# Soft-capped attention before two MLPs on one core: scores made with the keys on the partitions by two row tiles, exp with no row maximum, key sums by matmuls

## The chip, the cores and the metric

The kernel runs on 1 core of one Trainium2 chip. The metric is the device time of one execution in microseconds (us), the median over runs. The engines are TensorE (PE in the profile; PEld is its weight load), VectorE (DVE), ScalarE (ACT), GpSimd (POOL) and SyncE (SP, which issues most of the DMAs).

## The reference

Attention over 4 batches, 12 heads, 448 tokens and a head size of 64, in float32; then one MLP with relu squared and one with x·sigmoid(1.702x), both 768 → 2048 → 768, on the 1792 tokens. `cap` is 30; the weights are float64.

```python
scores = scale * np.matmul(q, k.transpose(0, 1, 3, 2))
scores = cap * np.tanh(scores / cap)
scores = scores - np.max(scores, axis=-1, keepdims=True)
attn = np.exp(scores)
attn = attn / (np.sum(attn, axis=-1, keepdims=True) + 1e-09)
x = np.matmul(attn, v)                      # heads side by side: [1792, 768]
h = np.maximum(x @ w_in, 0.0);  x = h * h @ w_out
h = x @ w_in2;  out = (h * (1.0 / (1.0 + np.exp(-1.702 * h)))) @ w_out2
```

## The kernel before, in words

A float32 operand is split as hi + lo in the type float32r, and a product of two such operands is three float32r matmuls (hi·hi, hi·lo, lo·hi), or two where one side's halves lie side by side.

**Attention** goes by pairs of heads (24 pairs, 6 for each batch). q and k of a pair are transposed to [64 x 2 heads, tokens], by TensorE for batches 0 and 1 and by VectorE's 32x32 transposes for batches 2 and 3 (`DVE_QK`). k's halves are written once for each head and copied to the other 64 partitions by a DMA on GpSimd's queue (`prep_k`, step 3), so that a score matmul contracts over 128 rows: q's hi and lo of one head against k's hi, and again against k's lo. `scores` puts the queries on the partitions (112 at a time). ScalarE takes tanh out of PSUM (`tanhs`), VectorE takes each row's maximum (`row_max`), ScalarE takes exp of 448 elements at a time with the maximum as bias and the row sum as accumulated output (`exps`), VectorE divides by the sum (`norm`). TensorE then transposes the probabilities (`trans`, 16 transposes for a head, four of them with 64 output partitions), ScalarE and VectorE take them from PSUM and split them (`take`), and `pv` multiplies with v. For batch 0 (`PLAIN_PV`) that product is left in float32.

**The MLPs** go by units of work n: 68 units for a batch, each one product of 15 or 18 matmuls of 448 columns (`product`), in all 1152 matmuls for a batch. The weights come as float64 halves in batch 0, are brought to float32 by ScalarE (`rebias`) and VectorE (`join`), written back to DRAM by SP (`keep`), and split by both (`split_w`). Later batches read `keep`.

**The order.** `HEAD_PLAN` and `PAIR_PLAN` say in which quarter slot of a head a step is issued; `attn_sub(t)` issues one quarter slot. The attention of batch 0 stands alone, ahead of the first product; that of batch s + 1 is issued between the units of batch s. Each engine then works its instructions off in order. SP's queue takes the loads of q, k, v, the weights and the `keep` writes in the order of issue.

Of the kernel before, what the change touches and what calls it, by code (L numbers as in the profile page):

```python
# [8 lines left out]
F32 = mybir.dt.float32  # L9
F32R = mybir.dt.float32r  # L10
I32 = mybir.dt.int32
U8 = mybir.dt.uint8
# [9 lines left out]
def softcap_attention_mlp_mlp(ctx, tc, q, k, v, cap, w1, w2, w3, w4, out):  # L22
    """Soft-capped attention, then a relu^2 MLP, then a x*sigmoid(1.702x) MLP.

    The weights are float64 and come as the int32 halves of their words. They are brought to
    float32 on chip once and kept in DRAM for the later batches.

    A float32 operand x is split exactly into x = hi + lo with hi = float32r(x), and a product is
    the sum of the float32r products hi*hi + hi*lo + lo*hi.

    """
# [14 lines left out]
    # batches whose product with v is left in float32  # L46
# [6 lines left out]
    # batches whose q and k are transposed on the vector engine  # L53
    DVE_QK = (2, 3)
    # pairs whose scores are left in float32
# [54 lines left out]
    def emit_const():  # L110
        nc.sync.dma_start(out=capt, in_=cap.rearrange("(o n) -> o n", o=1).to_broadcast([P, 1]))
        make_identity(nc, ident)
        for t in sx:
            nc.gpsimd.memset(t, 0)
        # tanh is odd: cap and -cap give the same scores
        nc.vector.tensor_scalar(ncap, capt, -1.0, None, ALU.mult)
        nc.vector.tensor_tensor(acap, capt, ncap, ALU.max)
        nc.vector.tensor_scalar(ncap, acap, -1.0, None, ALU.mult)
        nc.vector.reciprocal(qs, acap)
        nc.vector.tensor_scalar(qs, qs, float(D) ** -0.5, None, ALU.mult)  # L120

# [5 lines left out]
    def load_pair(b, p):  # L127
        if b in DVE_QK:
            # blocks of 32 x 32, which the vector engine transposes in place
            qt = ld.tile([P, S // 32, 32], F32, tag="q", name="qt")  # L130
            kt = ld.tile([P, S // 32, 32], F32, tag="k", name="kt")
            for t, src in ((kt, k), (qt, q)):
                for j in range(4):
                    Q_LOAD.dma_start(
                        out=t[32 * j : 32 * j + 32],
                        in_=src[b, 2 * p + j // 2, :, 32 * (j % 2) : 32 * (j % 2) + 32].rearrange(
                            "(c p) d -> p c d", p=32
                        ),
                    )
        else:  # L140
            qt = ld.tile([CP, NCH, 2, D], F32, tag="q", name="qt")
            kt = ld.tile([CP, NCH, 2, D], F32, tag="k", name="kt")
            for t, src in ((kt, k), (qt, q)):
                for j in range(2):
                    Q_LOAD.dma_start(
                        out=t[:, :, j, :], in_=src[b, 2 * p + j].rearrange("(p c) d -> p c d", c=NCH)
                    )
        raw[b, p] = (qt, kt)

    def transposed(b, t, name):  # L150
        """[64 x 2 heads, tokens] of a pair's q or k."""
# [11 lines left out]
    def load_v(b, p):  # L163
        plain = b in PLAIN_PV
        if plain:
            # [v_even | 0 | v_odd], so that both heads of a pair add into one bank
# [16 lines left out]
    def split_v(b, p, half):  # L183
        if b in PLAIN_PV:
            return
        if half == 0:
            # [hi_even | lo_even | lo_odd | hi_odd]
# [123 lines left out]
    def take(b, h, half):  # L311
        """The transposed probabilities from PSUM."""
# [86 lines left out]
    # a quarter slot's work: what feeds an operation was made a quarter slot or more before  # L399
# [46 lines left out]
    def ready(b):  # L446
        """The quarter slot that ends the attention of batch b, and leaves ps_x free."""
        return 4 * (H * (b + 1) - 1) + LAST_HEAD + 1

# [1 line left out]
    layer = []  # L451
    for l, (wa, wb) in enumerate(((w1, w2), (w3, w4))):
# [11 lines left out]
        # the next group's first product stands ahead of a group's second ones  # L464
# [31 lines left out]
    def words(n, t):  # L496
        """A unit's raw words without their two lowest bytes, in elements of type t."""
        return wraw[n][:, : units[n][5], :].bitcast(t).rearrange("p k (f e) -> p k f e", f=P)

    def rebias(n):  # L500
        """float64 to float32, first part: the upper 13 bits.

        The upper 16 bits of a float64 are taken as a bfloat16 and cast to float16, which loses the
        three upper bits of the exponent: what is left are the upper 16 bits of the float32, the last
        three of them zero.
        """
# [5 lines left out]
    def join(n):  # L512
        """float64 to float32, second part: the lower 19 bits of the fraction."""
# [43 lines left out]
    def finish(n, part):  # L557
        """What follows a product, in two parts."""
# [3 lines left out]
        if kind == "a":  # L562
            if part == 0:
# [8 lines left out]
                else:  # L572
                    # h * sigmoid(1.702 h) = 0.5 h (1 + tanh(0.851 h)); the 0.5 comes at the end
# [9 lines left out]
        if part == 0:  # L583
# [4 lines left out]
            # the 0.5 of the second MLP's activation  # L588
# [28 lines left out]
    def ahead(n):  # L617
        """The weights' way ahead of unit n."""
# [5 lines left out]
    def urgent(n):  # L624
        """Whether the unit after n takes what n gives."""
# [50 lines left out]

# [28 lines left out]
```

## Time and profile before

| | us |
|---|---|
| median of 3 runs (1248.27 to 1251.95) | 1249.37 |
| the profiled execution, first to last instruction (its span) | 1247.7 |
| PE busy / DVE busy / ACT busy in the span | 1211.9 / 929.9 / 834.8 |

Only the span of the profiled execution is known; the median is 1.7 us longer than it. I cut the span where a batch's products begin and end:

| stage | from to (us) | what runs |
|---|---|---|
| A | 0 to 128.4 | attention of batch 0, and the first pairs of batch 1 |
| B | 128.4 to 430.1 | MLPs of batch 0, attention of batch 1, weights from float64 |
| C | 430.1 to 722.5 | MLPs of batch 1, attention of batch 2 |
| D | 722.5 to 1007.1 | MLPs of batch 2, attention of batch 3 |
| E | 1007.1 to 1247.7 | MLPs of batch 3, alone |

A matmul's duration in the profile (about 0.37 us) is longer than the distance from one to the next (about 0.205 us), because matmuls follow each other through the array. So PE's busy time says little of how much work it has; the distances between starts do.

### The profile page before, as it was taken

To read this page: it belongs to the slowest core of one execution; us is meant where nothing else is said; L and a number is where in the kernel's file an instruction comes from. 1 tells how busy PE (TensorE), PEld (TensorE's weight loads), DVE (VectorE), ACT (ScalarE), POOL (GpSimd) and SP (SyncE) were. 2 spreads that over 40 slices of the span, in tenths; PEclk is the share of its full clock that TensorE was granted. 3 is DMA by queue.
4 is the path that set the end of the run, shared out by engine and by line. 5 is a ranking of instruction groups with operands and counts; after the bars stand their busy time and mean duration, and the time that the engine had idled before them with its cause. 6 is when DMAs were issued, how large, how long until landed. Compare 5 with 4: busy or idle time off the path is not lost.

```text
span 1247.7 us, 17463 instructions
## 1 busy us (share of the span) xinstructions
PE 1211.9 (97%) x6192; PEld 1096.6 (88%) x6192; DVE 929.9 (75%) x1497; ACT 834.8 (67%) x1459; POOL 74.7 (6%) x140
## 2 busy tenths in 40 slices
PE   4998999989999999999999999999999999999997
PEld 3676898879999999999999999999999999999997
DVE  5999987979989986789768876778745663565354
ACT  6999988888987776677766847667654443344332
POOL 2000000000000310000000130000000130000000
PEclk9999999989999999999999999999999999999999
DMA  6734898879888864334334353232222243233232
GB/s 149 196 68 128 268 285 235 273 210 296 243 280 246 264 166 120 110 100 138 116 88 127 94 163 109 71 100 102 77 93 93 99 151 109 98 114 120 97 108 50
DMA packets 188039, 185.67 MB, mean 149 GB/s; under 512 B 109744, under 2 KB 158896, under 8 KB 187952
## 3 DMA queue, kind: packets, MB, share of 16 engines
q1 hardware_dynamic: 177776, 168.72, 44.4%
q0 software_dynamic: 4608, 15.15, 4.8%
q10 hardware_dynamic: 5568, 0.69, 0.3%
q8 instruction: 49, 0.80, 0.3%
q14 instruction: 38, 0.31, 0.1%
HBM read 142.84 MB, written 30.67 MB: 139 GB/s over the span
## 4 chain that ended last, share of the span: by engine, by line
PE 81%; DVE 7%; ACT 6%; DMA 3%; issue 1%; SPq 0%; DVEq 0%; ACTq 0%
PE mps L552 68%; PE tps L305 5%; PE sps L257 4%; PE vps L370 3%; DMA wraw<-in_moe_w_out_dram 2%; ACT e L284 2%; DVE st L278 1%; DVE e L295 1%; ACT sx L510 1%; PE vps L365 1%; DVE y L517 1%; ACT wh L534 1%; DVE qq L240 1%; DVE wl L536 1%; DMA wraw<-in_moe_w_in_dram 1%
## 5 line engine op out<-in xcount | busy, mean ns | idle before, releaser
L552 PE MATMUL mps<-g,wh 128*128 128x448 f32 x1536 | 443.6, 370 | 6.0 <-ACT g L579 4.0
L552 PE MATMUL mps<-xt,wh 128*128 128x448 f32 x1536 | 440.7, 368 | 2.5 <-ACT wh L534 2.5
L534 ACT ACTIVATE wh<-wraw 128x768 fp32r<-128x768 f32 (+1 forms) x204 | 164.6, 807 | 263.1 <-PE mps L552 237.1
L552 PEld LDWEIGHTS mps<-g,wh 128*128 128x128 f32 x1536 | 287.5, 189 | 32.4 <-ACT g L579 4.7
L552 PEld LDWEIGHTS mps<-xt,wh 128*128 128x128 f32 x1536 | 286.5, 188 | 26.4 <-ACT wh L534 2.7
L536 DVE TENSOR_TENSOR wl<-wraw,wh 128x768 fp32r<-128x768 f32 (+1 forms) x204 | 185.0, 907 | 160.6 <-ACT wh L534 157.3
L552 PE MATMUL mps<-g,wl 128*128 128x448 f32 x768 | 282.0, 367 | 1.0 <-DVE wl L536 1.0
L552 PE MATMUL mps<-xt,wl 128*128 128x448 f32 x768 | 281.0, 366 | 0.0
L284 ACT ACTIVATE e<-e,st,acap 112x448 f32<-112x448 f32 x192 | 144.1, 752 | 20.2 <-DVE st L280 19.8
L552 PEld LDWEIGHTS mps<-g,wl 128*128 128x128 f32 x768 | 144.9, 189 | 13.5 <-DVE wl L536 1.4
L552 PEld LDWEIGHTS mps<-xt,wl 128*128 128x128 f32 x768 | 144.2, 188 | 12.1
L579 ACT ACTIVATE g<-r 128x448 fp32r<-128x448 f32 x128 | 73.6, 575 | 56.1 <-DVE r L575 29.5
L305 PEld LDWEIGHTS tps<-ident,e 112*128 112x128 f32 (+1 forms) x768 | 98.2, 183 | 12.5 <-ACT e L273 4.2
L278 DVE TENSOR_REDUCE st<-e 112x2 f32<-112x896 f32 x96 | 103.0, 1079 | 7.8 <-ACT e L273 7.5
L257 PE MATMUL sps<-kk,qq 128*112 128x448 f32 x384 | 101.5, 387 | 6.4 <-DVE qq L240 2.1
L305 PE MATMUL tps<-ident,e 112*128 112x112 f32 (+1 forms) x768 | 103.7, 276 | 1.5 <-ACT e L273 1.1
L581 DVE TENSOR_TENSOR g<-r,g 128x448 fp32r<-128x448 f32 x128 | 79.4, 620 | 32.2 <-ACT g L579 31.5
L593 DVE SCALAR_TENSOR_TENSOR y<-mps,y 128x448 f32<-128x448 f32 x96 | 59.5, 619 | 53.1 <-PE mps L552 52.4
L273 ACT ACTIVATE e<-sps 112x896 f32<-112x896 f32 x96 | 87.3, 912 | 9.2 <-PE sps L257 7.1
L257 PEld LDWEIGHTS sps<-kk,qq 128*112 128x112 f32 x384 | 67.0, 179 | 22.6 <-ACT e L273 4.1
L510 ACT ACTIVATE sx<-wraw 128x768 f16<-128x768 bf16 (+1 forms) x68 | 69.8, 1029 | 19.2 <-DMA wraw<-in_moe_w_out_dram 9.1
L295 DVE TENSOR_SCALAR e<-e,st 112x448 f32<-112x448 f32 x192 | 78.7, 450 | 1.7
(73 smaller groups left out, 1150.9 us busy)
## 6 DMA issues: line engine op xcount, KB each, us to landing
wraw<-keep SPq DMA_DIRECT2D x66, 768.0 KB, 4.3
wraw<-in_moe_w_in_dram SPq DMA_DIRECT2D x32, 766.5 KB, 5.7
wraw<-keep SPq DMA_DIRECT2D x36, 640.0 KB, 4.3
keep<-y SPq DMA_DIRECT2D x44, 384.0 KB, 3.4
wraw<-in_moe_w_out_dram SPq DMA_DIRECT2D x24, 638.8 KB, 5.5
kk<-kk POOLq DMA_DIRECT2D x48, 224.0 KB, 3.6
wraw<-in_moe_w_out_dram SPq DMA_DIRECT2D x12, 766.5 KB, 6.3
keep<-y SPq DMA_DIRECT2D x24, 320.0 KB, 3.1
```

Source lines behind the costliest of these rows:

```text
L257: nc.tensor.matmul(ps[:CP, u, :S], qq[:, j, c * CP : (c + 1) * CP], kk[:, j, i, :], start=(i == 0), stop=(i == 1),)
L273: nc.scalar.activation(e[:, 2 * half : 2 * half + 2, :], ps[:CP, :, :S], AF.Tanh)
L278: nc.vector.tensor_reduce(st[:, 0, cs], e[:, cs, :], axis=AX.X, op=ALU.max)
L284: nc.scalar.activation(e[:, c, :], e[:, c, :], AF.Exp, scale=acap[:CP], bias=st[:, 1, c : c + 1], accum_out=st[:, 2, c : c + 1],)
L295: nc.vector.tensor_scalar(e[:, c, :], e[:, c, :], st[:, 3, c : c + 1], None, ALU.mult)
L305: nc.tensor.transpose(ps[:n, u, c * CP : (c + 1) * CP], e[:, c, cols], ident[:CP, :CP])
L510: nc.scalar.activation(z, words(n, BF16)[:, :, :, 2], AF.Copy)
L534: nc.scalar.activation(hi[:, :kn], t[:, :kn], AF.Copy)
L536: eng.tensor_tensor(lo[:, :kn], t[:, :kn], f32(hi[:, :kn]), ALU.subtract)
L552: nc.tensor.matmul(ps[:, :S], a[:, kk, :], r, start=(kk == 0 and i == 0), stop=(kk == kn - 1 and i == 2),)
L579: nc.scalar.activation(g[:, 0, :], r, AF.Copy)
L581: eng.tensor_tensor(g[:, 1, :], r, f32(g[:, 0, :]), ALU.subtract)
```

## The change

The old kernel stays as a function `any_cap`, for caps over 40. A new function `bounded_cap` computes the same for caps up to 40, and a branch at the end runs `any_cap` as well if the cap is larger (here it is 30, so the branch is not taken). In `bounded_cap`:

- `scores` puts the keys on the partitions and the queries along the columns, for both heads of a pair. Each matmul contracts over the 64 rows of one head: the even head's lie in rows 0 to 63 of the array, the odd head's in rows 64 to 127, and they write to two PSUM banks. Three products (hi·hi, hi·lo, lo·hi) for each head and chunk of 112 keys make 6 matmuls for each `scores` call and 24 for a pair. The copy of k to the other partitions is gone.
- `exps` takes exp with no maximum, 896 elements at a time. `row_max`, `norm`, `trans` and `take` are gone: the probabilities already lie as `pv` wants them, and are split there (`split_hi`, `split_lo`).
- The sums over the keys are matmuls with a column of ones, for batch 0 from every chunk (`PE_SUMS`), for the others from the chunks added up on VectorE (`add_keys`). Their reciprocals are spread over the 64 rows of a head by another matmul and multiplied to the product with v (`recip`, `normalize`).
- q and k of batch 1 are transposed on VectorE too, and v is split in all batches.

```diff
+    DVE_QK = (1, 2, 3)
+    PE_SUMS = (0,)
+    NORM = {0: [(0, 3), (3, 5), (5, 6)]}
+    DVE_HI = {0: (0, 2)}
...
+    def scores(b, p, c):
+
+        qq, kk = prep[b, p]
+        ps = sc[b, p, c] = ps_s.tile([P, 2, 512], F32, tag="s", name="sps")
+        for i, (ik, iq) in enumerate(((0, 0), (0, 1), (1, 0))):
+            for j in range(2):
+                r = slice(64 * j, 64 * j + 64)
+                nc.tensor.matmul(
+                    ps[:CP, j, :S], kk[r, ik, c * CP : (c + 1) * CP], qq[r, iq, :],
+                    start=(i == 0), stop=(i == 2),
+                )
+
+    def tanhs(b, p, c):
+        e = et[b, p, c] = e_p.tile([CP, 2, S], F32, tag="e", name="e")
+        nc.scalar.activation(e, sc.pop((b, p, c))[:CP, :, :S], AF.Tanh)
+
+    def exps(b, p, c):
+        e = et[b, p, c]
+        nc.scalar.activation(e, e, AF.Exp, scale=ecap[:CP])
+
+    def split_hi(b, p, c):
...
+        if c in DVE_HI.get(b, ()):
+            nc.vector.tensor_copy(hi, e)
+        else:
+            nc.scalar.activation(hi, e, AF.Copy)
+
+    def split_lo(b, p, c):
+        hi, lo = hl[b, p, c]
+        nc.vector.tensor_tensor(lo, et[b, p, c], f32(hi), ALU.subtract)
+
+    def add_keys(b, p, c):
...
+        nc.vector.tensor_tensor(a, et[b, p, 0] if c == 1 else a, et[b, p, c], ALU.add)
+
+    def key_sum(b, p, c):
...
+        for j in range(2):
+            w = one[:CP, P - 1 - row - j : 2 * P - 1 - row - j]
+            for n, t in enumerate((hi, lo)):
+                nc.tensor.matmul(
+                    ps[:, :S], w, t[:, j, :],
+                    start=first and j == 0 and n == 0, stop=last and j == 1 and n == 1,
+                )
+
+    def pv(b, p, c):
...
+        for j in range(2):
+            a = vt[:, c, 2 * j : 2 * j + 2, :].rearrange("p a d -> p (a d)")
+            for n, t in enumerate((hi, lo)):
+                nc.tensor.matmul(
+                    pvp[b, p][j][:, :S], a, t[:, j, :],
+                    start=(c == 0 and n == 0), stop=(c == NCH - 1 and n == 1),
+                )
+        if b in PE_SUMS:
+            key_sum(b, p, c)
...
+    def recip(b, p, step):
...
+            nc.vector.reciprocal(sums[r], sums[r])
+        elif step == 1:
+            nc.scalar.activation(rcp[r, 0, :], sums[r], AF.Copy)
+        elif step == 2:
+            nc.vector.tensor_tensor(rcp[r, 1, :], sums[r], f32(rcp[r, 0, :]), ALU.subtract)
+
+    def normalize(b, p, k):
...
+            for m in range(2):
+                nc.tensor.matmul(
+                    ps[:, u, :S],
+                    spread[n - p0].rearrange("p j d -> p (j d)"),
+                    rcp[:, m, :],
...
+            x = x32[b, n]
+            nc.vector.tensor_tensor(x, x, ps[:, u, :S], ALU.mult)
+            if b == 0:
+                split_x(b, n)
...
+        11: [(sum_hi,)],
+        12: [(take_x, 0), (take_x, 1), (sum_lo,), (recip, 0)],
+        13: [(sum_keys,), (recip, 1)],
+        14: [(take_sums,), (recip, 2)],
+        15: [(recip, 3)],
+        16: [(recip, 4)],
+        17: [(normalize, 0)],
+        18: [(normalize, 2)],
+        19: [(normalize, 4)],
+    }
+    for c in range(NCH):
+        for i, f in enumerate((scores, tanhs, exps, split_hi, split_lo, pv)):
+            PLAN.setdefault(2 * c + i, []).append((f, c))
+        PLAN[2 * c + 4].append((add_keys, c))
...
+    nc.sync.dma_start(out=c[:, 0:1], in_=cap.rearrange("(o n) -> o n", o=1))
...
+    nc.vector.tensor_scalar(over, c[:, 0:1], CAP_MAX, None, ALU.is_gt)
+    bounded_cap(tc, q, k, v, cap, w1, w2, w3, w4, out)
+    flag = nc.values_load(over, min_val=0, max_val=1)
+    with tc.If(flag > 0):
+        any_cap(tc, q, k, v, cap, w1, w2, w3, w4, out)
```

The order of TensorE's matmuls in stage B, at a place where attention stands between the products (`mps`) of batch 0's MLPs; before, with `vps` the product with v, `tps` the transposed probabilities and `qps` q transposed:

```order
L552 MATMUL mps<-g,wl 128x448
L158 MATMUL qps<-ident,qt 128x112 x4
L370 MATMUL vps<-pb,vs 128x448 x2
L370 MATMUL vps<-pc,vs 128x448
L305 MATMUL tps<-ident,e 128x112 x4
L305 MATMUL tps<-ident,e 64x112 x4
L552 MATMUL mps<-g,wh 128x448 x2
```

And now, with `sps` the scores and `sums` the sums over the keys (the product is line 1185, the scores line 888):

```order
L1185 MATMUL mps<-g,wl 128x448
L888 MATMUL sps<-qq,kk 112x448 x6
L956 MATMUL vps<-phi,vs 128x448
L956 MATMUL vps<-plo,vs 128x448
L956 MATMUL vps<-phi,vs 128x448
L956 MATMUL vps<-plo,vs 128x448
L888 MATMUL sps<-qq,kk 112x448 x6
L942 MATMUL sums<-phi,one 128x448
L1185 MATMUL mps<-g,wh 128x448 x2
```

The transposes are gone from between the products; a run of 6 score matmuls, each on half of the array's rows, and matmuls on all 128 rows take turns.

The order of ScalarE's instructions late in stage A; before, with line 273 the tanh, line 284 the exp, 337 a copy of transposed probabilities, 396 the split of x, 215 and 191 the splits of k and v:

```order
L284 ACTIVATE e,st<-e,st,acap 112x448
L273 ACTIVATE e<-sps 112x896
L284 ACTIVATE e,st<-e,st,acap 112x448
L396 ACTIVATE xt<-x_1046 128x448
L337 ACTIVATE pb<-tps 128x448
L215 ACTIVATE kk<-kps 64x448 x2
L191 ACTIVATE vs<-vraw 128x4x2x64
L273 ACTIVATE e<-sps 112x896
L284 ACTIVATE e,st<-e,st,acap 112x448 x3
```

And now, with line 895 the tanh, 899 the exp, 909 the hi half of the probabilities, 974 the product with v taken from PSUM, 1014 the hi half of the reciprocals:

```order
L895 ACTIVATE e<-sps 112x896
L974 ACTIVATE ct<-vps 64x448 x2
L899 ACTIVATE e<-e,ecap 112x896
L895 ACTIVATE e<-sps 112x896
L909 ACTIVATE phi<-e 112x896
L899 ACTIVATE e<-e,ecap 112x896
L895 ACTIVATE e<-sps 112x896
L862 ACTIVATE kk<-kps 128x448
L899 ACTIVATE e<-e,ecap 112x896
L1014 ACTIVATE rcp<-sums 4x448
```

There is one exp for 896 elements where there were two of 448, and it waits for the tanh alone, where before it waited for VectorE's maximum; the copies of the transposed probabilities are gone, the hi halves and the copies `ct` are new.

## Rows read from the trace of the kernel before

**Rows 1.** The page: engines' busy time, and the chain that ended last.

```profile
PE 1211.9 (97%) x6192; PEld 1096.6 (88%) x6192; DVE 929.9 (75%) x1497; ACT 834.8 (67%) x1459; POOL 74.7 (6%) x140
PE 81%; DVE 7%; ACT 6%; DMA 3%; issue 1%; SPq 0%; DVEq 0%; ACTq 0%
```

**Rows 2.** Busy time by stretch: 40 us within stage A, then stages A to E.

```profile
core 0: us, PE busy (x) PEld busy (x) DVE busy (x) ACT busy (x) POOL busy (x), PEclk, DMA share, GB/s
40.00:80.00 40.00, 38.84 (x203) 27.75 (x202) 39.00 (x78) 39.70 (x80) 4.32 (x12) 1.00 0.48 115
0.00:128.40 128.40, 104.87 (x517) 76.92 (x517) 111.31 (x214) 114.44 (x221) 13.77 (x38) 0.96 0.54 136
128.40:430.10 301.70, 295.74 (x1529) 271.50 (x1529) 268.98 (x420) 257.82 (x437) 13.74 (x24) 0.99 0.85 262
430.10:722.50 292.40, 292.40 (x1526) 270.09 (x1525) 232.96 (x387) 201.46 (x364) 21.47 (x36) 1.00 0.43 121
722.50:1007.10 284.60, 284.60 (x1475) 262.29 (x1474) 196.29 (x309) 166.87 (x292) 18.19 (x30) 1.00 0.31 101
1007.10:1247.70 240.60, 234.31 (x1153) 215.81 (x1151) 120.36 (x170) 94.19 (x148) 7.51 (x12) 1.00 0.33 104
```

**Rows 3.** Products alone (line 552), in stages B to D together and in E.

```profile
128.40:1007.10 878.70, 736.58 (x3454) 645.92 (x3455) 1.00 0.54 163
1007.10:1247.70 240.60, 234.31 (x1153) 215.81 (x1151) 1.00 0.33 104
```

**Rows 4.** Stages B to D, line by line: scores (L257), transposed probabilities (L305), product with v (L370).

```profile
128.40:1007.10 878.70, 62.35 (x256) 44.46 (x256) 1.00 0.54 163
128.40:1007.10 878.70, 70.61 (x551) 69.35 (x550) 1.00 0.54 163
128.40:1007.10 878.70, 67.44 (x245) 45.79 (x245) 1.00 0.54 163
```

**Rows 5.** Timeline of PE in stages C and D: start, us, then the instructions.

```profile
692.53 1.07 PE L305 MATMUL tps<-ident,e 112*128 112x112 f32 x8
693.38 0.64 PE L552 MATMUL mps<-xt,wh 128*128 128x448 f32 x2
...
766.66 0.37 PE L552 MATMUL mps<-g,wl 128*128 128x448 f32 x1
766.86 0.98 PE L257 MATMUL sps<-kk,qq 128*112 128x448 f32 x4
767.68 0.57 PE L552 MATMUL mps<-g,wh 128*128 128x448 f32 x2
```

**Rows 6.** Timeline where transposes into 64 columns of the array end and products begin.

```profile
605.25 0.77 PE L305 MATMUL tps<-ident,e 112*128 112x112 f32 x6
605.37 0.42 PEld L305 LDWEIGHTS tps<-ident,e 112*64 112x64 f32 x4
...
605.80 0.65 PE L552 MATMUL mps<-xt,wh 128*128 128x448 f32 x2
```

**Rows 7.** Groups of ScalarE's and VectorE's instructions over the span, shapes apart.

```profile
L284 ACT ACTIVATE e<-e,st,acap 112x448 f32<-112x448 f32 x192 | 144.1, 752 | 20.2 <-DVE st L280 19.8
L278 DVE TENSOR_REDUCE st<-e 112x2 f32<-112x896 f32 x96 | 103.0, 1079 | 7.8 <-ACT e L273 7.5
L273 ACT ACTIVATE e<-sps 112x896 f32<-112x896 f32 x96 | 87.3, 912 | 9.2 <-PE sps L257 7.1
L284 ACT ACTIVATION_READ_ACCUMULATOR e<-e,st,acap 112x1 f32 x192 | 36.5, 190 | 0.0
L534 ACT ACTIVATE wh<-y 128x768 fp32r<-128x768 f32 x44 | 36.8, 836 | 3.4 <-PE mps L552 1.6 <-DVE y L517 0.9 <-ACT pc L342 0.8
L536 DVE TENSOR_TENSOR wl<-y,wh 128x768 fp32r<-128x768 f32 x44 | 41.9, 952 | 6.1 <-ACT wh L534 5.8
L579 ACT ACTIVATE g<-r 128x448 fp32r<-128x448 f32 x128 | 73.6, 575 | 56.1 <-DVE r L575 29.5 <-DVE r L571 25.8
L581 DVE TENSOR_TENSOR g<-r,g 128x448 fp32r<-128x448 f32 x128 | 79.4, 620 | 32.2 <-ACT g L579 31.5
```

More of the change, by code (lines that the diff above doesn't have):

```diff
@@ L21, in softcap_attention_mlp_mlp, with any_cap @@
 @with_exitstack
-def softcap_attention_mlp_mlp(ctx, tc, q, k, v, cap, w1, w2, w3, w4, out):
+def any_cap(ctx, tc, q, k, v, cap, w1, w2, w3, w4, out):
     nc = tc.nc
@@ new lines, with softcap_attention_mlp_mlp @@
+CAP_MAX = 40.0
+@with_exitstack
+def softcap_attention_mlp_mlp(ctx, tc, q, k, v, cap, w1, w2, w3, w4, out):
+    nc = tc.nc
+    pool = ctx.enter_context(tc.tile_pool(name="flag", bufs=1))
+    c = pool.tile([1, 2], F32, name="capsize")
+    over = pool.tile([1, 1], I32, name="over")
+    nc.sync.dma_start(out=c[:, 0:1], in_=cap.rearrange("(o n) -> o n", o=1))
+    nc.vector.tensor_scalar(c[:, 1:2], c[:, 0:1], -1.0, None, ALU.mult)
+    nc.vector.tensor_tensor(c[:, 0:1], c[:, 0:1], c[:, 1:2], ALU.max)
+    nc.vector.tensor_scalar(over, c[:, 0:1], CAP_MAX, None, ALU.is_gt)
[3 more added lines that the diff above has]
+        any_cap(tc, q, k, v, cap, w1, w2, w3, w4, out)
```

445 lines of the change are left out of this document (added).

## The prediction

> **What bounds the kernel now.** I read the page first: PE is busy 97% of the span, and 81% of the chain that ended last is PE [rows 1]. An average over stages with different limits says little, so next come the busy times by stretch [rows 2]. In stage A two other engines are full: in 40 us of it ACT is busy 39.7 and DVE 39.0. A lasts 128.4 us, of which ACT works 114.4 and waits 14.0, mostly while the first loads come. In C and D PE never idles, with DVE at 69 to 80% and ACT lower: there each PE instruction removed is time gained. B is PE's as well but for 6 us of idleness; its DMA share of 0.85 is the next limit. E is products alone.
>
> The price of a product comes from E: 234.3 us for 1153 matmuls, 0.2032 us each [rows 3]. In B to D the 3454 products cost 702 us of 878.7. The attention between them is 256 score matmuls, 551 transposes and 245 matmuls with v [rows 4]. From one start to the next, four scores take 0.82 us (0.205 each) and eight transposes 0.85 us (0.106 each) [rows 5]; with v at 0.205 that makes 52.5 + 58.4 + 50.2 = 161.1 us. The remaining 15 us are waits, q and k transposes, and stretches at the lower clock.
>
> **Stages B to D: PE.** The built program, in its order of issue, has 402 score matmuls behind the fifth product, and 392 full-height ones: 282 with v, 72 sums, 38 that spread reciprocals. The 392 have a known shape, 392 × 0.205 = 80.4 us. The transposes are gone. The 402 are of a kind that the trace doesn't show: 64 rows each, in pairs for the two halves of the array. Bounds: if the halves work at once, a pair can't be faster than one matmul's 0.205 us; if they take turns, a pair takes 0.41. For the issue of two weight loads and two matmuls the nearest row is the transposes, each a load and a matmul in 0.106 us, so 0.21 for two. I take 0.22 for a pair: 201 × 0.22 = 44.2 us.
>
> A rule on packing would put it higher. The Trainium skill (TensorE: Matmul & The Clock Gate, section Measured speedup vs the span model) gives 3.07 times for four row tiles; by the same share of the ideal two would take an estimated 0.27 us a pair, and the whole forecast would be 10 us longer. No row here shows it.
>
> The runs of scores and the full-height matmuls change the way the array is divided 141 times behind the fifth product. The nearest row is the change from transposes into 64 columns of the array back to products: the first product starts at 605.80, while the transposes before it end at 605.25 + 0.77 = 606.02 [rows 6]. So the array wasn't emptied first. I take 0.025 us for a change, 3.5 us; the upper bound is that the array empties each time, 0.37 − 0.205 = 0.165 us, by the length of a matmul less its distance [rows 5].
>
> B to D then hold 44.2 + 80.4 + 3.5 = 128.1 us of attention instead of 161.1: **−33 us**, between −40 and +2 by the bounds of the pair. The 15 us of waits I leave. In B the DMA engines bound this: 0.85 × 301.7 = 256 us of work [rows 2]. The copies of k (two for a pair) go, but batch 1's q and k come in pieces of 128 bytes instead of 256; I take that as even. B stays far above 256 us: by its share of the counts (84 pairs of scores, 160 others) it falls by 2 us alone, since work that stood in A comes into it; C falls by 19 and D by 12. DVE and ACT lose row maximum, division and copies in these stages, so the cover that hides them grows.
>
> **Stage A: ACT and DVE.** Up to the fifth product the new order has 27 tanh, 27 exp, 15 hi copies on ACT, 43 instructions of about 448 elements and 6 for weights; before it was 32 tanh, 60 exp with the reading of the sum, 8 copies of 896, 53 small ones and 8 for weights. So part of the gain is that fewer pairs of batch 1 stand ahead of the first product; that work is in B's count above. Prices [rows 7]: tanh 0.912; old exp 0.752 + 0.190; small 0.575; weights 0.84; hi copy over 896 from 0.575 at 448 and 0.836 at 768, on the same line 0.94. The new exp over 896 lies between the tanh's 0.91 and twice the old 0.752, nearest the first, since one instruction's fixed part falls away: 1.04. Before: 29.2 + 56.5 + 7.3 + 30.5 + 6.7 = 130 us against 114.4 measured, since neighbours overlap, a factor 0.88. After: 24.6 + 28.1 + 14.1 + 24.7 + 5.0 = 96.5, times 0.88 = 85 us.
>
> DVE: 25 lo halves at 1.08 (0.952 for 768, 0.620 for 448), 12 hi copies between 0.62 and 1.08 (I take 0.9), some 57 small ones at 0.62, 10 others about 5 us: 27 + 11 + 35 + 5 = 78 us against 111.3. The reciprocal over 448 elements no row shows; it stands in the small ones, and three of them at several times 0.62 would add 6 us and leave DVE below ACT. PE: 87 pairs × 0.22, 208 matmuls × 0.205, 48 transposes, changes: 68 us.
>
> ACT stays the fullest. With the old 14 us of waiting, A would take 99 us. I don't take that: the sums of the last pairs go through copy, reciprocal, hi, lo, spreading matmul, multiply and split, seven steps of about 0.6 us where there was one copy and the split, and each step queues behind other work on its engine. A new wait lies there too: `pv` of the next pair needs the two PSUM banks that `take_x` empties, and behind it on PE stand scores that ACT's tanh waits for; two slots, some 3 us, cover it. Between 99 and the old 128 I take 108, nearer to 99 because ACT held 99% and DVE 98% under the same in-order queues [rows 2]: **−20 us**, with −29 and 0 as ends. What is late next there is the weights' way to the first product, which costs nothing if its loads stand early on SP's queue, as they do in the new order.
>
> **Ends.** The tiny load of the cap stands first on SP's queue and delays q and k by one issue; the k copy's wait falls away: even. At the end each engine reads the flag and branches, SP behind the last stores. No row shows it; between nothing and a small load with its landing, some 5 us, I take **+2**.
>
> Sum: −33 − 20 + 2 = −51, on the profiled span of 1247.7 gives 1196.7; with the 1.7 us by which the median lies above the span, **1198 us**. About 0.3% (3.7 us) is what a measurement here can tell from no change.
>
> **Rivals.**
> *The array empties at each change between half and full height* (12%). For it speaks that 64-row tiles are a division that the trace doesn't show; against it rows 6, for columns. 141 × 0.14 = 20 us more in B to D, 2 in A: 1220. The Trainium skill states just that (TensorEngine Tiling (Array Packing), Key Properties: "Mode switching requires drain"); rows 6 disagree for the division by columns.
>
> *The halves take turns* (13%): then the change doesn't do what its name says. 402 × 0.205 + 80.4 = 163 us, nothing gained in B to D; PE in A rises to 85 us, level with ACT, which I price at 4 us: −16 + 2 + 2 gives 1237.
>
> *Slower* (7%): a 64-row matmul waits for what runs in the other rows, so that it costs its length rather than its distance. It decides at 402 × c + 80.4 − 16 + 2 = 161.1, c = 0.24 us a matmul. Turns plus emptying at both ends of a run of six is 0.26: 1259. The full 0.37 for each is +68 us in B to D and A unchanged: 1319. Against it: all matmuls in the trace follow at their distance, not their length.
>
> *Stage A gains nothing* (6%): ACT or DVE waits on the longer chains between three engines; the rest as forecast: 1218.
>
> The forecast has 62%. Its own range is 1185 to 1212, from A between 99 and 116 and the pair between 0.205 and 0.25. The range for 8 in 10 goes from 1181, A at its lower end and pairs with free changes, to 1240, which takes in emptying, A without gain and most of the turns; outside are the slower case and the tails of the others. Faster by over 0.3%: 0.62 + 0.12 + 0.06 and all but 3 of the 13 for turns, 0.90. Within 0.3%: 0.04, those 3 and a sliver of the slower case. Slower: 0.06.
>
> **What would show it.** The first run of products should begin near 108 us, with ACT full ahead of it. In C, six scores between two products should take about 0.7 us from the first start to the next other matmul; 1.2 would be turns, and 0.15 more at each end emptying. B should last about 299 us, C 274, D 272, E 235 for its products plus some 8. DMA share in B should stay under 0.92. The prediction is wrong if PE idles in C or D (a PSUM buffer or a lo half late), if B is held by weights, or if A stays over 120 us.

## The result, and the profile after

The changed kernel takes 1216.74 us (median of 4 runs, 1212.74 to 1223.88) against 1249.61 us for the kernel before on the same chip (1248.27 to 1251.95): a ratio of 0.9742, 95% interval 0.9705 to 0.9778. It is faster by 33 us, where 51 were forecast. The profiled execution is the slowest of the four, with a span of 1222.1 us.

The page of the kernel after, its busy times and the chain that ended last, beside [rows 1]:

```profile
PE 1189.1 (97%) x5832; PEld 1027.5 (84%) x5832; DVE 848.5 (69%) x1155; ACT 783.9 (64%) x1129; POOL 48.4 (4%) x83
PE 68%; DVE 1%; ACT 1%; DMA 0%; issue 0%; DVEq 0%; ACTq 0%
```

Busy time by stretch of the kernel after, for stages A to E; the columns are those of [rows 2]:

```profile
core 0: us, PE busy (x) PEld busy (x) DVE busy (x) ACT busy (x) POOL busy (x), PEclk, DMA share, GB/s
0.00:110.40 110.40, 95.53 (x432) 63.54 (x432) 77.85 (x112) 88.74 (x119) 3.13 (x11) 0.94 0.47 112
110.40:422.30 311.90, 303.24 (x1482) 257.70 (x1481) 268.61 (x353) 262.58 (x372) 10.17 (x16) 0.99 0.82 249
422.30:700.80 278.50, 278.50 (x1395) 245.74 (x1394) 199.60 (x274) 176.59 (x256) 12.55 (x20) 1.00 0.42 114
700.80:976.60 275.80, 275.80 (x1377) 244.77 (x1377) 182.34 (x248) 161.84 (x235) 15.11 (x25) 1.00 0.31 98
976.60:1222.10 245.50, 236.07 (x1153) 215.73 (x1152) 120.06 (x169) 94.18 (x148) 7.48 (x12) 0.99 0.34 102
```

| stage | before | forecast | after |
|---|---|---|---|
| A | 128.4 | 108 | 110.4 |
| B | 301.7 | 299 | 311.9 |
| C | 292.4 | 274 | 278.5 |
| D | 284.6 | 272 | 275.8 |
| E with the end | 240.6 | 243 | 245.5 |

A fell by 18 us, C and D by 23 together, but B, which took over work from A, rose by 10. PE still never idles in C and D. So the excess there lies in what PE's instructions cost, and the timeline of PE in stage C shows where (start, us, then the instructions; compare the scores in [rows 5]):

```profile
501.91 0.36 PE L1185 MATMUL mps<-g,wl 128*128 128x448 f32 x1
502.21 0.86 PE L888 MATMUL sps<-qq,kk 64*112 64x448 f32 x6
503.00 0.68 PE L1185 MATMUL mps<-g,wh 128*128 128x448 f32 x2
503.51 0.36 PE L1185 MATMUL mps<-g,wl 128*128 128x448 f32 x1
```

Six scores take 0.79 us from their first start to the next product. The distance ahead of them (from the start of the product before to their first start) is 0.30 us where 0.20 is usual between products, and the two products behind them take 0.51 where 0.41 is usual. So a run of six costs PE 0.79 + 0.10 + 0.10 = 0.99 us; the forecast had 3 × 0.22 + 2 × 0.025 = 0.71. Within the run the six starts come in three pairs, 3 or 4 ns apart, at 0, 0.29 and 0.50 us: two matmuls do start together.

B has something else besides. The timelines of PE and DVE there (the bracket is idle time before the row, and its releaser):

```profile
413.65 0.36 PE L956 MATMUL vps<-plo,vs 112*128 112x448 f32 x1
417.95 0.93 PE L1185 MATMUL mps<-xt,wh 128*128 128x448 f32 x2 [3.94 <-DVE y L1225]
...
416.65 0.65 DVE L1239 STREAM_TRANSPOSE o<-y 128x448 f32<-128x448 f32 x1 [4.49 <-DMA out_dram<-o]
417.22 0.58 DVE L1225 SCALAR_TENSOR_TENSOR y<-mps,y 128x448 f32<-128x448 f32 x1
```

DVE's transpose of an output tile waits 4.49 us until the store out of the same buffer has landed (the stores of 380 to 425 us take 2.7 us to land in the median, and 10.0 at most); behind it in DVE's queue stands the addition that empties a PSUM bank, and PE waits 3.94 us for that bank. From 418.1 to 421.5 the granted clock is then 0.50, and the products follow each other at 0.37 us. The rows of that spell and of the time when the store was under way (columns as above):

```profile
410.00:414.00 4.00, 4.00 (x21) 2.82 (x20) 2.17 (x3) 1.79 (x4) 1.72 (x3) 1.00 0.92 290
418.10:421.50 3.40, 3.40 (x10) 2.77 (x11) 3.40 (x5) 0.00 (x0) 2.00 (x4) 0.50 0.69 98
```

### The profile page after: what moved, and what is told of

The parts are those of the page before. It is cut to its first block, busy times and chain, and to the rows that moved or that the text cites. A ratio compares the mean times of both kernels' runs of the same rounds, so it can differ in the third digit from the quotient of the medians.

```text
span 1222.1 us, 15714 instructions
## 1 busy us (share of the span) xinstructions
PE 1189.1 (97%) x5832; PEld 1027.5 (84%) x5832; DVE 848.5 (69%) x1155; ACT 783.9 (64%) x1129; POOL 48.4 (4%) x83
## 4 chain that ended last, share of the span: by engine, by line
PE 68%; DVE 1%; ACT 1%; DMA 0%; issue 0%; DVEq 0%; ACTq 0%
PE mps L1185 61%; PE vps L956 3%; PE sps L888 3%; PE sums L942 1%; PE rps L1026 1%; DMA kt<-in_k_dram 0%; DVE y L1225 0%; DVE plo L913 0%; DVE wl L1169 0%; DVE y L1151 0%; ACT wh L1168 0%; ACT xt L1041 0%; DVE o L1239 0%; ACT sx L1144 0%; ACT e L895 0%
## 5 line engine op out<-in xcount | busy, mean ns | idle before, releaser
L1168 ACT ACTIVATE wh<-wraw 128x768 fp32r<-128x768 f32 (+1 forms) x204 | 164.8, 808 | 279.3 <-PE mps L1185 268.0
L1185 PEld LDWEIGHTS mps<-g,wl 128*128 128x128 f32 x768 | 145.1, 189 | 16.5 <-DVE wl L1169 4.0
L913 DVE TENSOR_TENSOR plo<-e,phi 112x896 fp32r<-112x896 f32 x96 | 103.8, 1081 | 13.8 <-ACT phi L909 13.0
L899 ACT ACTIVATE e<-e,ecap 112x896 f32<-112x896 f32 x96 | 99.7, 1040 | 1.3
L888 PE MATMUL sps<-qq,kk 64*112 64x448 f32 x576 | 92.1, 409 | 3.8 <-ACT qq L874 1.9
L1241 POOL DMA_DIRECT2D out_dram<-o x72 | 45.3, 636 | 942.1 <-DVE o L1239 941.3
L909 ACT ACTIVATE phi<-e 112x896 fp32r<-112x896 f32 x84 | 79.6, 947 | 4.2 <-PE vps L956 2.9
L888 PEld LDWEIGHTS sps<-qq,kk 64*112 64x112 f32 x576 | 45.6, 177 | 41.3 <-issue 17.9
L956 PE MATMUL vps<-phi,vs 112*128 112x448 f32 x192 | 73.1, 392 | 2.7 <-ACT phi L909 1.5
L956 PE MATMUL vps<-plo,vs 112*128 112x448 f32 x192 | 70.9, 384 | 2.1 <-DVE plo L913 2.1
```

Of the source, the lines that this page charges most:

```text
L888: nc.tensor.matmul(ps[:CP, j, :S], kk[r, ik, c * CP : (c + 1) * CP], qq[r, iq, :], start=(i == 0), stop=(i == 2),)
L899: nc.scalar.activation(e, e, AF.Exp, scale=ecap[:CP])
L909: nc.scalar.activation(hi, e, AF.Copy)
L913: nc.vector.tensor_tensor(lo, et[b, p, c], f32(hi), ALU.subtract)
L956: nc.tensor.matmul(pvp[b, p][j][:, :S], a, t[:, j, :], start=(c == 0 and n == 0), stop=(c == NCH - 1 and n == 1),)
L1168: nc.scalar.activation(hi[:, :kn], t[:, :kn], AF.Copy)
```

## The experiments

Unless said otherwise, each edit is made to the changed kernel. The runs were made on several chips, each beside the kernel before, so that the ratios compare better than the medians. Stages are counted here from the starts of the first product and of those numbered 1153, 2305 and 3457 in the profiled execution; by this count the changed kernel's own profile has 108.5, 313.7, 278.5 and 275.8 us for A to D. "Full clock from" is when the granted clock first rises from 1.2 to 2.4 GHz, and the last column how long it falls back to 1.2 within A and until when.

| run | median us (lowest, highest) | ratio to before | A | B | C | D | full clock from | half again in A |
|---|---|---|---|---|---|---|---|---|
| again | 1216.2 (1212.0, 1222.4) | 0.9724 (0.9691–0.9758) | 105.0 | 313.1 | 278.5 | 275.6 | 18.0 | 13.7, to 72.6 |
| turns | 1220.7 (1216.5, 1225.2) | 0.9760 (0.9724–0.9795) | 110.6 | 310.9 | 279.4 | 275.7 | 25.6 | 13.7, to 76.8 |
| full6 | 1220.5 (1220.0, 1221.1) | 0.9761 (0.9732–0.9789) | 101.0 | 311.8 | 283.5 | 279.4 | 16.5 | 3.4, to 64.2 |
| double12 | 1282.4 (1278.0, 1286.4) | 1.0245 (1.0208–1.0283) | 126.3 | 326.6 | 300.6 | 287.1 | 15.3 | twice 6.8 |
| onehalf | 1266.5 (1258.8, 1274.3) | 1.0130 (1.0076–1.0183) | 118.8 | 318.5 | 291.2 | 286.2 | 38.8 | none |
| paired | 1205.8 (1199.7, 1211.3) | 0.9643 (0.9617–0.9670) | 99.6 | 307.5 | 278.7 | 268.9 | 17.9 | none |
| ob3 | 1212.0 (1208.7, 1219.9) | 0.9677 (0.9653–0.9701) | 111.8 | 308.1 | 278.5 | 275.5 | 35.0 | 10.2, to 79.3 |
| noflag | 1211.9 (1208.9, 1214.9) | 0.9680 (0.9660–0.9700) | 103.1 | 309.3 | 278.5 | 275.6 | 16.0 | 10.2, to 70.7 |
| warm | 1211.8 (1211.1, 1215.2) | 0.9674 (0.9653–0.9695) | 102.9 | 311.0 | 278.6 | 275.9 | 8.1 | 10.2, to 69.5 |
| paired_ob3 | 1207.3 (1204.7, 1212.8) | 0.9636 (0.9611–0.9661) | 105.0 | 307.1 | 281.0 | 269.0 | 18.0 | 13.7, to 72.7 |
| lessdve | 1215.3 (1212.4, 1216.5) | 0.9694 (0.9670–0.9718) | 103.7 | 311.1 | 279.5 | 275.5 | 16.9 | 10.2, to 71.5 |
| paired_warm | 1204.1 (1198.9, 1209.1) | 0.9620 (0.9591–0.9648) | 99.7 | 307.5 | 279.3 | 268.9 | 8.4 | 3.4, to 63.0 |

**again: the kernel as it is.** No edit.

> The changed kernel itself, without an edit, as the base of the comparisons and to see how its executions scatter. Its first four times went from 1212.7 to 1223.9 us, the profiled one the highest. If the stall of 3.9 us on PE near 414 us and the half-speed spell behind it belong to that execution alone, this profile has a stage B nearer to 305 than to 312 us; if they are the kernel's own, they are there again.

The second profile repeats the first: B 313.1 us, the same wait of 4.4 us for the output buffer with 3.7 us of PE behind it, the same spells at half clock. So they aren't an accident of one execution. Their size does change: in noflag and warm below, whose edits don't touch B, DVE waits 2.0 and 2.2 us for the buffer and PE 1.5 and 1.7, and B takes 309.3 and 311.0 us. C agrees within 0.1 us. What differs is A, 105.0 against 108.5, and executions again scatter over 10 us.

**turns: one head's three scores, then the other's.**

```diff
-        for i, (ik, iq) in enumerate(((0, 0), (0, 1), (1, 0))):
-            for j in range(2):
+        for j in range(2):
+            for i, (ik, iq) in enumerate(((0, 0), (0, 1), (1, 0))):
```

> The same six score matmuls in another order: the three of one head, then the three of the other, so that two neighbours in the queue use the same half of the array. Theory (the halves work at once in the changed kernel): a run of six goes from about 1.0 us to six at 0.205 and the two changes, 1.4 us; over the 67 runs behind the first product that is some 28 us, 1245 us. Rival (the halves bring nothing, or take turns already): no change, 1217.

The expectation of 1245 failed: 1220.7, an interval that overlaps that of again, and C 0.9 us longer for its 21 runs. The timeline of PE in stage C:

```profile
501.82 0.37 PE L1185 MATMUL mps<-g,wl 128*128 128x448 f32 x1
502.12 0.87 PE L888 MATMUL sps<-qq,kk 64*112 64x448 f32 x6
502.92 0.69 PE L1185 MATMUL mps<-g,wh 128*128 128x448 f32 x2
```

It is the run of 0.80 us once more, its starts in pairs 10 ns apart. Either the halves bring nothing, as the rival has it, or the theory is right about the halves and wrong that the order in the queue matters.

**onehalf: both heads' scores in the same half.**

```diff
-                r = slice(64 * j, 64 * j + 64)
+                r = slice(0, 64)
```

> All six score matmuls of a run use rows 0 to 63: the second head gets the first head's scores, so the output isn't the reference's; number, size and places of the instructions stay. The exchange of the order (three of one head, then three of the other) changed nothing, the starts stayed in pairs. Theory (the two halves work at once, and each half takes its own matmuls from the queue): with one half alone no two can run together, six starts about 0.2 us apart, a run of 1.2 us and the changes, +0.4 us for each of the 67 runs behind the first product, about 1243. Rival (a matmul over 64 rows takes 0.1 us whichever half it uses, and the pairs come of something else): the starts stay in pairs and the time at 1216.

This decides it. The timeline of PE in stage C:

```profile
510.84 0.37 PE L1185 MATMUL mps<-xt,wl 128*128 128x448 f32 x1
511.14 1.46 PE L888 MATMUL sps<-qq,kk 64*112 64x448 f32 x6
512.53 0.67 PE L1185 MATMUL mps<-g,wh 128*128 128x448 f32 x2
```

A run takes 1.39 us, its starts are 0.20 us apart and none come in pairs; the widened distance at either end stays (0.30 ahead). B to D are 28.7 us longer than in again, as the theory says (+0.4 us for 67 runs, 27). The halves do work at once, in whichever order their matmuls stand in the queue. The rest of the 50 us is A's 13.8 and what other executions have more than the profiled one, which was among the shorter (1259.9); its clock rose late, as the rows under warm show.

**full6: six scores over all 128 rows.**

```diff
-                r = slice(64 * j, 64 * j + 64)
+                r = slice(0, 128)
```

> Six score matmuls over all 128 rows in place of six over 64: each head's scores then hold the sum over both heads, so the output isn't the reference's; no number or size of instructions changes. No change of the array's division is left and no two run at once. Theory (a change of division costs about 0.1 us at each end): six at 0.205, 1.23 us from the first start to the next other matmul with no widened distance around it, where the changed kernel has 1.0; 67 runs by 0.24 less the 0.1 at the entry, +10 to +16 us, 1227 to 1233. Rival (the widened distances come from something else that scores bring, their weight loads or the two PSUM banks): they stay, 1.4 us a run, about 1245.

In stage C:

```profile
504.46 0.37 PE L1185 MATMUL mps<-g,wl 128*128 128x448 f32 x1
504.67 1.37 PE L888 MATMUL sps<-qq,kk 128*112 128x448 f32 x6
505.88 0.57 PE L1185 MATMUL mps<-g,wh 128*128 128x448 f32 x2
```

1.21 us, and the distances at both ends are the usual 0.20: the widened ones belong to the change between 64 and 128 rows and not to weight loads or PSUM banks. C and D grow by 4.9 and 3.8 us, 0.22 for each of 39 runs, as expected. The whole grows by 4 us only, not by 10 to 16: A is 4.0 us shorter, with 3.4 us at half clock instead of 13.7, B is 1.3 shorter and the last products 2.2. The higher clock isn't that of the profiled execution alone: all four of full6 were granted 0.997 or 0.998 over their span, and the ten of the changed kernel (those of the result and of again) 0.989 to 0.994. So the six slower matmuls give back in the clock a part of what they cost.

**double12: each run twice.**

```diff
-        for i, (ik, iq) in enumerate(((0, 0), (0, 1), (1, 0))):
+        for i, (ik, iq) in enumerate(((0, 0), (0, 1), (1, 0)) * 2):
...
-                    start=(i == 0), stop=(i == 2),
+                    start=(i % 3 == 0), stop=(i % 3 == 2),
```

> Every run of scores is issued twice into the same banks, each time starting the sums anew: twelve matmuls instead of six, the same result. It parts the price of a pair from that of a change. Theory (0.2 to 0.25 us a pair and some 0.28 us once for a run): three more pairs cost 0.62 to 0.74 us, 67 runs make +41 to +49 us, 1258 to 1266 with stage A some 10 us longer at most. Rival (a pair costs a third of the run, 0.33 us, and a change nothing): 1.0 us more for a run, +67 us, 1284 and above.

```profile
507.07 0.37 PE L1185 MATMUL mps<-g,wl 128*128 128x448 f32 x1
507.37 1.47 PE L888 MATMUL sps<-qq,kk 64*112 64x448 f32 x12
508.77 0.68 PE L1185 MATMUL mps<-g,wh 128*128 128x448 f32 x2
509.28 0.36 PE L1185 MATMUL mps<-g,wl 128*128 128x448 f32 x1
```

In stage C three more pairs make the run 1.40 us instead of 0.79, **0.203 us a pair**, and leave its ends as they were. A run of six is therefore 0.61 us of work and 0.99 − 0.61 = 0.38 for its two changes: **0.19 us a change**, as the mean of the two. The time of 1282 misses the theory's 1258 to 1266 and looks like the rival's 1284, but isn't that: D, where the number of runs is 18 as before, grows by 11.5 us, 0.64 a run. The rest comes from A, 21 us longer, and from B and C, since the order of issue moved (C has 24 runs there instead of 21).

**paired: two blocks of keys in one run.** `TWO` issues the scores of blocks 1 and 3 together with those of 0 and 2; `LATE` moves the key sums and the reciprocals by one step and the spreading of the reciprocals by one to four.

```diff
...
+    TWO = {(scores, 1): 0, (tanhs, 1): 2, (scores, 3): 4, (tanhs, 3): 6}
+    PLANS = [PLAN] * (NP + 1) + [moved(LATE)] + [moved({**LATE, **TWO})] * (len(pairs) - NP - 2)
...
-                for f, *a in PLAN[d]:
+                for f, *a in PLANS[n].get(d, ()):
```

> From the third pair of batch 1 on, the scores of two blocks of keys are issued one behind the other, twelve matmuls in a run, at half as many places; the key sums and the spread of the reciprocals come one to four steps later, to leave both PSUM slots free. The work is the same. Theory (each run pays some 0.38 us for its two changes of the array's division, whatever its length): 28 runs fewer, -11 us, 1205. Rival (the widened distances belong to each block of keys, not to the change): nothing, 1216. If the later sums or the second PSUM slot hold PE up, it is slower than 1216, and PE shows waits at the scores in stages C and D.

1205.8 us, 10.5 below again in median, and the ratios' intervals lie apart. In stage C a run of twelve shows the 1.40 us again:

```profile
499.62 1.48 PE L888 MATMUL sps<-qq,kk 64*112 64x448 f32 x12
501.02 0.67 PE L1199 MATMUL mps<-g,wh 128*128 128x448 f32 x2
```

B, C and D together take 855.2 us instead of 867.2, where 28 runs fewer at 0.38 us make 10.6. That the two are close is in part chance: in this profile B also lacks again's 3.7 us wait and its 6.8 us at half clock, and other small waits have come, some of them in C and D (1.2 us of PE's idle time, where again has none). Beside ob3, which lacks the long wait as well, the ratio is lower by 0.0034 only, some 4 us. What the run of twelve shows is the price, 0.38 us for each run saved; how much of the 10 us is due to it, the medians don't part. A, which the edit doesn't reach, was 5.4 us shorter in the profiled execution, with no half-speed spell.

**ob3: three output buffers**, and one buffer fewer for the attention's result, to make room.

```diff
-    X32B = 7
+    X32B = 6
-    OB = 2
+    OB = 3
```

> Three buffers for the output tile instead of two, and six instead of seven for the attention's result, to make room. Both profiles of the changed kernel show PE waiting 3.7 to 3.9 us near 410 us for an update on DVE, which itself stands behind the transpose of an output tile whose buffer is still being stored, and a half-speed spell of 3.4 us behind that. Theory (that wait is a part of what stage B takes beyond the forecast): the wait and the spell go, -4 to -5.5 us, 1211. Rival (DVE and the DMA queues are late there anyway): the wait moves to the next weights, and the time stays at 1216.

The wait for the buffer is gone from the chain of waits, with PE's wait and the spell behind it, and B falls from 313.1 to 308.1 us. The median falls by 4.2; the intervals of the ratios overlap a little (0.9691 and 0.9701), so that the stage shows it better than the median does. Not all of B's 5 us need be the buffer's: noflag, with two buffers, has 309.3 and still a wait of 1.5 us on PE.

**lessdve: two thirds of batch 1's additions left out.**

```diff
-        if b in PE_SUMS or c == 0:
+        if b in PE_SUMS or c == 0 or (b == 1 and c > 1):
```

> In batch 1 the exps of key blocks 2 and 3 aren't added to the key sums, so batch 1's denominators lack half their terms and the output isn't the reference's; twelve DVE instructions of 1.07 us go from stage B, of DVE's 269 us there, and nothing else. Theory (stage B's waits come from DVE being late, as it stands behind most of PE's waits there): B goes from 311 to 313 us to 303 to 306, the time to 1208. Rival (the waits come from the DMA of the stores, from ACT and from the lower clock behind each stall): B stays over 309.

B is 311.1 us, though DVE does some 11 us less there (258.7): the rival's figure holds. DVE's wait for the output buffer fell from 4.4 to 0.9 us, and with it PE's idle time in B from 8.5 to 5.2; the rest of that idle time, 5 us in ob3 too, isn't set by how much DVE has to do.

**noflag: the bounded kernel alone.**

```diff
-    flag = nc.values_load(over, min_val=0, max_val=1)
-    with tc.If(flag > 0):
-        any_cap(tc, q, k, v, cap, w1, w2, w3, w4, out)
```

> The bounded kernel alone, without the load of the flag, the branch and the other kernel behind it; the tiny load of the cap stays. Theory (the ends cost what the forecast says and a bit more): the stretch from the last product to the end goes from 8.8 to about 5.6 us, -3 us, 1213. Rival (the code of the branch costs elsewhere, as loads of instructions): more than 5 us. If the end stays at 8.8 us, the 3 us belong to something else, such as the stores.

The last matmul of the kernel after, with its span, and the last of noflag with its own:

```profile
core 0 of [0], span 1222.1 us
1213.35 0.36 PE L1185 MATMUL mps<-g,wl 128*128 128x448 f32 x1
```

```profile
core 0 of [0], span 1207.0 us
1201.40 0.37 PE L1185 MATMUL mps<-g,wl 128*128 128x448 f32 x1
```

From its start to the end it is 8.7 us with the branch and 5.6 without, 3.1 us for the flag and the branch. The median falls by 4.3, though the intervals of the ratios overlap a little.

**warm: matmuls without use while PE waits.**

```diff
+        def warm(count):
+            ps = ps_m.tile([P, 512], F32, tag="m", name="warm")
+            for _ in range(count):
+                nc.tensor.matmul(ps[:, : 2 * P], one[:, :P], one, start=True, stop=True)
...
             attn_sub(T)
+            if T in (-8, -5):
+                warm(13 if T == -8 else 9)
```

> Twenty-two matmuls without use (128 rows, 256 columns, of a constant tile into a bank that nobody reads) stand where PE waits for the first q and for its copies, 13 behind the first transposes of k, 9 behind those of q. Over the eight profiles so far in which only the scores or something far from stage A differ, the first product starts between 99.6 and 118.8 us, and its start follows the granted clock: where the full 2.4 GHz is granted from 16 to 18 us on, it starts at 99.6 to 105; where from 25.6 to 38.8, at 108.5 to 118.8. Theory (much of the scatter and of stage A's length is PE at the lower clock, after its idle spells at the start): the clock is granted by 16 us, the first product starts at 98 to 105, the median falls by 3 to 6 us to 1211 and the scatter narrows. Rival (the clock rises when it does, whatever PE did before): the same scatter, 1216 or a microsecond more for the delay.

Busy time from 20 to 40 us of again, warm and onehalf, in this order, columns as above:

```profile
20.00:40.00 20.00, 20.00 (x107) 13.85 (x106) 13.70 (x17) 19.43 (x26) 0.00 (x0) 1.00 0.80 214
```

```profile
20.00:40.00 20.00, 19.48 (x105) 13.33 (x104) 14.74 (x19) 19.93 (x27) 0.00 (x0) 1.00 0.81 222
```

```profile
20.00:40.00 20.00, 20.00 (x53) 13.05 (x52) 7.62 (x9) 10.01 (x12) 0.00 (x0) 1.00 0.42 109
```

Onehalf's PE is busy throughout and does 53 matmuls, 0.38 us each, where the others do 105 to 107; ACT is busy for half the time and DVE for less. The column of the clock says 1.00, but it knows the clock only from its first change on (38.8 us there), so the distances tell it. Warm has the full clock from 8.1 us, its first product at 102.9, a median of 1211.8 and a scatter of 4 us instead of 10. The ratio's interval touches that of again, and the spell at 59 us is still there: in both profiles with these matmuls (8.1 us here, 8.4 in paired_warm) the clock rose early, but the spell stayed. Noflag, whose clock rose at 16.0 us, has its first product at 103.1, so a rise earlier than that isn't seen to bring more.

**paired_ob3 and paired_warm.** The edits are those above.

> The paired runs of scores together with the third output buffer. Paired alone gave 1205.8 us, the third buffer alone 1212.0, against 1216.2 for the changed kernel in the first call. Theory: both gains stand beside each other, 1201 to 1203. Rival: the later steps of the paired order have removed the wait for the output buffer already (its trace shows none there), so the second brings nothing, 1205.

> The paired runs of scores and the twenty-two matmuls without use at the start, without the third output buffer, which brought the paired order nothing. Theory (the two act in different places, the changes of division behind the first product, the clock ahead of it): 10 to 11 us and some 4 us below the changed kernel's 1216, 1200 to 1203, with a scatter of 5 us or less. Rival (the paired order's executions at 1200 to 1204 had the clock early already, so that the early clock lifts only the slow ones): the lowest time stays at 1199 to 1200 and the median comes to about 1203.

The third buffer adds nothing to the paired order (1207.3): that order had no wait for the buffer. Paired_warm, at 1204.1 us and a ratio of 0.9620, is the fastest of all and beats both kernels, but it can't be told from paired; its lowest time is paired's, as the rival said, and its scatter stayed at 10 us, so that warm's narrow scatter isn't shown to come from the early clock.

## Why the prediction was right, and where it was not

**The sign and the range** held: 1216.7 lies between 1181 and 1240. The forecast of 1198 was 19 us too low, and the step that failed has a name: the 0.025 us for a change of the array's division, taken from the transposes into 64 columns in [rows 6]. Those cost nothing visible; the change between 64 and 128 rows costs 0.19 (full6, double12). That is the price of the first rival, "the array empties at each change", which had 12% and 1220 us: the likeliest case was the wrong one. Its 0.165, by length less distance, was a little short. That the array empties is not shown: the first scores start at 502.21, before the modelled end of the product ahead of them at 502.27. The Trainium skill's sentence on it, that changing the tiling mode drains TensorE (TensorEngine Tiling (Array Packing), Key Properties), agrees with the cost at a change of rows, and not with [rows 6] for a change of columns.

**The pair** was forecast at 0.22 us and takes 0.203, one matmul's distance, its lower bound. By the Trainium skill's speedup of 3.07 for four row tiles (TensorE: Matmul & The Clock Gate, Measured speedup vs the span model) the prediction estimated 0.27; the trace disagrees with that for two. With the measured prices the row tiles' term is 201 × 0.203 + 141 × 0.19 = 67.6 us where 47.7 stood, and these 20 us are about what the median missed by (18.7). So the largest term of the sum came out at much less than it said: B to D fell by 12.5 us together where 33 stood, and most of the gain is A's 18.

**Turns** (13%) and **slower** (7%) are out: pairs start 3 or 4 ns apart, and onehalf shows what it is when they don't. **Stage A gains nothing** (6%) is out by A's 18 us.

**C and D** came out at 278.5 and 275.8 for 274 and 272. 21 and 18 runs by the 0.28 us that a run costs more make 6 and 5; PE never idles there.

**B**, 311.9 for 299: some 28 runs by 0.28 explain 8. Of the other 5, PE's idle time makes 2.7: it is 8.7 us in B, and 6.0 in [rows 2]. The half-clock time there is as it was (6.8 us, before 6.9), and the remaining 2 us are open. "The 15 us of waits I leave" was wrong here in that the waits didn't stay: the longest before, 4.0 us for a tile `g` of ScalarE, is gone, and the 3.9 us behind the output buffer came. DVE has 269 us of work in B as before, so the cover that was to grow there didn't, but lessdve shows that its amount sets little of B beyond the wait for the buffer. The DMA share fell to 0.82, under 0.92 as forecast; the store was late all the same. From 410 to 414 us the share was 0.92, which may be why; no run tests it. What sets the remaining small waits of B wasn't tried.

**A**, 110.4 for 108, was right in its prices. Groups of the kernel after:

```profile
L899 ACT ACTIVATE e<-e,ecap 112x896 f32<-112x896 f32 x96 | 99.7, 1040 | 1.3
L909 ACT ACTIVATE phi<-e 112x896 fp32r<-112x896 f32 x84 | 79.6, 947 | 4.2 <-PE vps L956 2.9
L913 DVE TENSOR_TENSOR plo<-e,phi 112x896 fp32r<-112x896 f32 x96 | 103.8, 1081 | 13.8 <-ACT phi L909 13.0
L907 DVE CAST phi<-e 112x896 fp32r<-112x896 f32 x12 | 7.4, 618 | 0.8 <-ACT e L899 0.8
L1012 DVE RECIPROCAL sums<-sums 12x448 f32<-12x448 f32 x3 | 8.8, 2936 | 0.0
```

Exp 1.040 for 1.04, hi copy 0.947 for 0.94, lo half 1.081 for 1.08; DVE's hi copy 0.618, the lower bound, where I took 0.9. The reciprocal takes 2.94 us where 0.62 stood, as the text feared, and the two cancel: DVE is busy 77.9 us for 78, ACT 88.7 for 85. But the 108 itself was in part luck. ACT isn't full ahead of the first product (80%), and PE runs a part of A at the lower clock: over the profiles with the same work in A the first product comes between 99.6 (full clock from 17.9 us and no spell) and 111.8 (from 35.0, and a spell of 10.2). Where the clock didn't fall again (paired), the first run of products begins at 101.4 us, near the 99 that the prediction worked out and didn't take; most of the 9 us that it added for longer chains were, by these profiles, the clock's. This is also what most of the scatter of the kernel's runs looks like. The granted clock is known for every execution, though only over the whole span and from its first change on: of the changed kernel's ten executions the four at 0.993 or 0.994 took 1212.0 to 1212.7 us, the six at 0.989 to 0.992 took 1216.3 to 1223.9. Only one execution of each run is profiled, so that how much of this is A's stays open.

**The ends** were sized at +2 and are +3.1. E's other 1.8 us aren't theirs: from the first to the last start its 1152 products take 236.7 us here, and 234.8 to 235.0 in the kernel before, turns, full6, paired and noflag; why, no run shows.

## What to carry to other kernels

Price a run of row-tiled matmuls as its pairs plus a fixed sum for entering and leaving the division, and so put as many of them in one run as PSUM holds; here that saves 0.38 us for each run that is joined to another. A price taken from a change of columns says nothing of a change of rows. When a change gives PE less to do in a stage that another engine bounds, look at the granted clock of that stage too: here the same stage took 99.6 to 111.8 us with the same work, and longer where more of it ran at 1.2 GHz.

## What the hardware showed that was not expected

- Two 64-row matmuls in different halves of the array start some 3 ns apart, and 10 ns in turns, even if they stand three places apart in the queue: in turns a run lasts 0.80 us. If they started in the order of the queue, the first half's three would start at 0, 0.2 and 0.4, the other's three from 0.4 on, and the next product at 1.0 at the earliest. The Trainium skill (TensorE: Matmul & The Clock Gate, The mechanism) says that matmuls start strictly in program order; the trace of turns disagrees for two row halves.
- A run's two changes between 64 and 128 rows cost 0.38 us, spread in parts of about 0.1 over the distances ahead of the first pair, behind it, behind the last pair, and behind the first product after it; none is seen for the change of columns in [rows 6].
- A DVE reciprocal over 448 elements takes 2.94 us on 12 partitions and 2.93 on 2.
- With the matmuls without use, which keep PE busy from 5.0 to 8.5 us, the full clock came at 8.1 us (warm) and 8.4 (paired_warm); without, at 15.3 to 38.8, and the two profiles of the same kernel differ in it (25.6 and 18.0).
